# Hedgehog linear attention feeding a squared-ReLU FFN: first loads in parts, maxima subtracted in two k groups, latencies of the plan changed for batch 0

## The chip, the cores and the metric

One core of a Trainium2 chip. The metric is device microseconds for one launch. Every number called a time is the median of a kernel's runs; a span or a time of day inside a run comes from one profiled execution of that kernel, which is 1.7 to 1.9 us shorter than the time that the same execution is given.

## The reference

```python
# q, k, v: 8 batches x 8 heads x 576 x 64;  w_phi: 64 x 128
def phi(x):
    proj = einsum('bhsd,df->bhsf', x, w_phi)
    proj = proj - max(abs(proj), axis=-1, keepdims=True)
    return concatenate([exp(proj), exp(-proj)], axis=-1)
q_p, k_p = phi(q), phi(k)
kv  = einsum('bhsf,bhsd->bhfd', k_p, v)          # "KV" below
z   = sum(k_p, axis=2)
num = einsum('bhsf,bhfd->bhsd', q_p, kv)         # numerator
den = einsum('bhsf,bhf->bhs', q_p, z)[..., None] + 1e-06
x   = (num / den).transpose(0, 2, 1, 3).reshape(4608, 512)
h   = maximum(x @ w_in, 0.0)                     # FFN-in, 512 -> 2048
out = h * h @ w_out                              # FFN-out, 2048 -> 512
```

## The kernel before

All inputs are loaded from f32 to bf16. The kernel does not emit its instructions in the order of the source text. It builds operations with an engine, an estimated cost, an estimated latency, dependencies, buffers and a priority key, simulates all engines, and then emits each operation in the order in which the simulation started it, so each engine gets its instructions in that order.

```python
class Plan:
    SWITCH = 96                       # planned cost of a change between 64- and 128-row matmuls
    AHEAD, GROUP, LATE = 12, 2, 4     # when to change the row size
    def pick(self, q, rows, can): ...
    def order(self):                  # event simulation: cost, latency, free buffers, priority
        ...
                    end, lat = now + o.cost, o.lat
                    if o.rows is not None:
                        if rows[e] not in (None, o.rows):
                            end += self.SWITCH
                        rows[e] = o.rows
        ...
    MARGIN = 200
    def pe(key, cost, fn, deps=(), bufs=(), rows=128):
        o = pl.op("pe", cost, key, fn, deps, bufs, lat=350, rows=rows)
        ...
    def act(key, n, fn, deps=(), bufs=()):
        return pl.op("act", 60 + 0.83 * n, key, fn, deps, bufs, lat=220 + MARGIN)
    # dve(): lat=190 + MARGIN;  pool(): lat=150 + MARGIN
    ...
    FIRSTS = "k0 v0 q0 win k1 v1 wout q1"    # batch 0 in two halves, the rest whole
```

The exponentials of k come in five groups a batch: four of 8 units and one of 4 (a unit is 128 tokens-by-head rows of 64). There are two ways to handle the maximum. In the first, here called folding, ScalarE takes the exponential of the raw projection straight from PSUM, and the factor exp(-max) or exp(+max) is multiplied onto v instead, once for each sign. In the second, VectorE subtracts the maximum, ScalarE takes both signs of two banks in two long instructions, and v is copied once, unscaled. Before the change batches 0 and 1 fold in all five groups, and later batches subtract in all of them.

```python
    FOLD, VON = 2, ((1, 1), (0, 1))    # VON[batch][sign]: 1 = GpSimd scales v, 0 = VectorE does
    ...
        fold = b < FOLD
        if not fold:                   # plain copy of v and its column of ones, on GpSimd
            ...
        for g, (u0, n) in enumerate(GRP):
            ...                        # projection of k: 64-row matmuls into two banks
            if not fold:
                ...                    # per bank: reduce abs max, subtract -> ksh (VectorE)
                ...                    # two exponentials of 2*c (ScalarE)
                continue
            ...                        # reduce abs max (VectorE), four exponentials of c (ScalarE)
            for s_, (y, sg) in enumerate(zip(va, (-1.0, 1.0))):
                ...                    # exp(sg * max), small (ScalarE)
                on = VON[b][s_]
                def fn(y=y, u0=u0, n=n, v_=(nc.vector, nc.gpsimd)[on]):
                    v_.tensor_tensor(
                        out=y.t[:, u0 : u0 + n, :D], in0=xv.t[:, u0 : u0 + n, :],
                        in1=y.t[:, u0 : u0 + n, D].to_broadcast([P, n, D]), op=ALU.mult)
```

Where the plan leaves the tensor engine (PE) idle before the first FFN input exists, it puts a matmul on a constant tile, a filler:

```python
    def warm():
        nc.tensor.matmul(out=r_one.tiles[7][:, : 2 * Fd], lhsT=ones[:, :P], rhs=ones, ...)
    ...
    pl.fill("pe", 108, lambda now: 500 if now < 500 else 240 if now < 5500 else PER, warm, o_end)
    ...
    with tc.manual_schedule():
        for o in pl.order():
            if o.fn is not None:
                o.fn()
```

## Time and profile before

| | before |
|---|---|
| time, us (first 3 runs) | 367.8 (367.53 to 368.38) |
| span of the profiled run | 365.6 |
| PE busy, of it fillers | 353.7, 16.4 (101 fillers) |
| first FFN-in matmul at | 28.11 |
| first FFN-out matmul at | 44.80 |
| clock in 43.4 to 46.8 us | 0.50 |

PE is TensorE, PEld its weight loads, DVE is VectorE, ACT is ScalarE, POOL is GpSimd, SP is SyncE; L and a number is a line of that kernel. Line numbers differ between the kernels: folded v is scaled at L523 before and L541 after, KV is L556 and L574, the numerators L700 and L720, FFN-in L762 and L782, FFN-out L791 and L811.

The prediction below shows the page and the table by stretches. Two more views belong to the argument. The first is the chain of work that ended last, by engine; the second, the PE waits between 28 and 49 us (engine, tile and line that waited, what it waited for, total us, times, longest).

```profile
PE 82%; DVE 6%; DMA 3%; POOL 3%; SPq 2%; issue 2%; ACT 1%; DVEq 0%; POOLq 0%; ACTq 0%
```

```profile
PE one L700 <- ACT kph L508: 1.3, 2, 0.7
PE one L466 <- DVE xo L721: 0.9, 1, 0.9
PE one L762 <- ACT hr L767: 0.2, 1, 0.2
```

The chain is 82% PE; VectorE, DMA and GpSimd hold 12% of it; that is where something other than PE set the pace. No single wait between 28 and 49 us is above 0.9 us: the loss there is made of small pieces. The timeline of the same stretch (start, duration, engine, line, operation) shows who scales v in batch 1.

```profile
36.07 1.05 POOL L523 TENSOR_TENSOR va<-xv,va 128x512 bf16<-128x512 bf16 x1
...
39.67 2.52 POOL L523 TENSOR_TENSOR va<-xv,va 128x512 bf16<-128x512 bf16 x2
40.06 1.21 DVE L523 TENSOR_TENSOR va<-xv,va 128x512 bf16<-128x512 bf16 x1
```

VectorE and GpSimd do the same kind of scaling at the same time. VectorE's scaling at 36.08 (shown in the prediction, 1.59 us) began with GpSimd's of 1.05 us and ended 0.55 us after it, at 37.67; the one at 40.06 ended at 41.27, also 0.54 after GpSimd's first of the pair, which ended at 40.73 by the single records. So 0.54 us is what it costs VectorE once the other is out of the way. GpSimd waits in its turn: its second of the pair, from 40.69, took 1.50 us in place of 1.05 and ended 0.92 after VectorE's at 41.27. This is what the Trainium skill, "SBUF — State Buffer", section Who interferes with whom, says of a VectorE instruction with two SBUF inputs beside a GpSimd one that reads SBUF, and the trace agrees: 1.59 = 1.05 + 0.54.

### The profile page before, as it was taken

What the parts mean: (1) busy time and instruction counts of PE and PEld (TensorE: products, weight loads), DVE (VectorE), ACT (ScalarE), POOL (GpSimd) and SP (SyncE); (2) the same over time, 40 slices, a digit from 0 to 9 for tenths busy, and PEclk for the clock granted to TensorE, in tenths of its full rate; (3) what the DMA queues carried; (4) which work ended last, traced back from release to release, by engine and by line L of the source; (5) the groups of instructions that cost most, each with busy time, mean ns of one, the idle gap of its engine ahead of it and who ended that gap; (6) DMA issues with size and microseconds to landing.
All of it is one profiled execution on the core that took longest, in us unless ns stands there. A gap on an engine that the chain in (4) does not pass through costs nothing.

```text
span 365.6 us, 10343 instructions
## 1 busy us (share of the span) xinstructions
PE 353.7 (97%) x4069; PEld 200.0 (55%) x4069; DVE 246.5 (67%) x553; ACT 242.3 (66%) x501; POOL 186.0 (51%) x289
## 2 busy tenths in 40 slices
PE   8899799999999999999999999999999999999994
PEld 6679576766654555455545554454445544444442
DVE  2779969894789589868596868875886743332321
ACT  2997979689739983997479846985699633333300
POOL 8855745458837881787538764785445600000000
PEclk9999899999999999999999999999999999999999
DMA  7999962559755975488656944595520331121133
GB/s 110 208 209 208 208 119 59 90 85 166 133 102 81 173 147 103 87 161 157 94 102 113 176 96 100 90 216 87 109 64 22 74 82 34 29 48 41 29 72 73
DMA packets 68257, 39.81 MB, mean 109 GB/s; under 512 B 48624, under 2 KB 63088, under 8 KB 68208
## 3 DMA queue, kind: packets, MB, share of 16 engines
q0 software_dynamic: 15312, 18.35, 30.3%
q1 hardware_dynamic: 52896, 20.79, 28.7%
q8 instruction: 32, 0.52, 0.6%
q14 instruction: 17, 0.14, 0.1%
HBM read 36.77 MB, written 9.44 MB: 126 GB/s over the span
## 4 chain that ended last, share of the span: by engine, by line
PE 82%; DVE 6%; DMA 3%; POOL 3%; SPq 2%; issue 2%; ACT 1%; DVEq 0%; POOLq 0%; ACTq 0%
PE one L791 32%; PE one L762 31%; PE one L700 6%; PE one L556 4%; PE one L600 3%; PE one L632 3%; DVE mk L477 2%; POOL va L523 2%; DMA xv<-in_v_dram 2%; DVE ksh L487 2%; PE one L466 2%; SPq L401 2%; DMA qT<-xq 1%; PE one L366 1%; DVE ot L798 1%
## 5 line engine op out<-in xcount | busy, mean ns | idle before, releaser
L770 POOL TENSOR_TENSOR h<-hr 128x512 bf16<-128x512 bf16 x112 | 115.8, 1042 | 87.1 <-ACT hr L767 85.0
L762 PE MATMUL one<-xT,win 128*128 128x512 bf16 (+2 forms) x768 | 145.7, 326 | 0.9 <-DVE ksh L487 0.7
L791 PE MATMUL one<-wout,h 128*128 128x512 bf16 x576 | 145.9, 381 | 0.2 <-DVE m L653 0.2
L767 ACT ACTIVATE hr<-one 128x512 bf16<-128x512 f32 x144 | 85.3, 606 | 77.8 <-PE one L762 69.6
L762 PEld LDWEIGHTS <-win 128*128 128x128 bf16 x768 | 66.0, 98 | 50.4 <-issue 1.8
L791 PEld LDWEIGHTS <-h 128*128 128x128 bf16 x576 | 51.8, 98 | 57.3 <-issue 2.6
L607 ACT ACTIVATE qph<-one 128x512 bf16<-128x512 f32 (+1 forms) x160 | 78.0, 572 | 7.0 <-PE one L600 5.8
L495 ACT ACTIVATE kph<-ksh 128x1024 bf16<-128x1024 f32 (+1 forms) x60 | 54.9, 969 | 11.4 <-DVE ksh L487 10.9
L477 DVE TENSOR_REDUCE mk<-one 128x4 f32<-128x512 f32 (+1 forms) x80 | 49.3, 625 | 5.5 <-PE one L466 5.5
L653 DVE TENSOR_REDUCE m<-one 128x4 f32<-128x512 f32 (+1 forms) x60 | 35.5, 628 | 18.6 <-PE one L632 12.8
L798 DVE COPY ot<-one 128x512 f32<-128x512 f32 x36 | 24.7, 686 | 27.1 <-PE one L791 26.8
L710 DVE TENSOR_TENSOR one<-one,em 128x260 f32<-128x260 f32 (+1 forms) x80 | 32.0, 430 | 13.2 <-PE one L700 11.0
L487 DVE TENSOR_TENSOR ksh<-one,mk 128x512 f32<-128x512 f32 (+1 forms) x60 | 38.3, 638 | 3.3
L700 PEld LDWEIGHTS <-qph 128*128 128x128 bf16 x640 | 30.1, 98 | 16.4 <-issue 3.2
L700 PE MATMUL one<-kv_sb,qph 128*128 128x65 bf16 x640 | 34.7, 194 | 1.3 <-ACT kph L508 1.3
L721 DVE TENSOR_TENSOR xo<-one,rden 128x256 bf16<-128x256 f32 (+1 forms) x80 | 31.3, 417 | 0.6
L773 DVE TENSOR_TENSOR h<-hr 128x512 bf16<-128x512 bf16 x32 | 13.5, 422 | 23.3 <-ACT hr L767 23.3
L662 POOL COPY mq<-m 64x4 f32<-64x4 f32 x108 | 20.0, 185 | 9.4 <-DVE m L653 5.6
L556 PE MATMUL one<-va,kph 64*128 64x65 bf16 x1152 | 23.9, 191 | 0.2
L556 PEld LDWEIGHTS <-kph 64*128 64x128 bf16 x1152 | 21.2, 94 | 4.9 <-issue 4.4
L508 ACT ACTIVATE kph<-one 128x512 bf16<-128x512 f32 (+1 forms) x40 | 19.6, 605 | 2.1 <-DVE mk L477 2.1
L366 PE MATMUL one<-ones 128*128 128x256 bf16 x101 | 16.4, 305 | 1.2 <-DVE scrap L312 1.2
(46 smaller groups left out, 209.1 us busy)
## 6 DMA issues: line engine op xcount, KB each, us to landing
out_dram<-ot SPq DMA_DIRECT2D x72, 128.0 KB, 2.4
xk<-in_k_dram POOLq DMA_DIRECT2D x7, 576.0 KB, 6.4
xv<-in_v_dram POOLq DMA_DIRECT2D x7, 576.0 KB, 9.0
xq<-in_q_dram POOLq DMA_DIRECT2D x7, 576.0 KB, 11.8
win<-in_moe_w_in_dram POOLq DMA_DIRECT2D x1, 2048.0 KB, 18.8
wout<-in_moe_w_out_dram POOLq DMA_DIRECT2D x1, 2048.0 KB, 29.8
xk<-in_k_dram POOLq DMA_DIRECT2D x2, 288.0 KB, 5.3
xv<-in_v_dram POOLq DMA_DIRECT2D x2, 288.0 KB, 7.5
```

The source lines that it names most:

```text
L477: nc.vector.tensor_reduce(out=mk.t[:, e, ms], in_=wv(e), axis=AX.X, op=ALU.max, apply_absolute_value=True)
L487: nc.vector.tensor_tensor(out=ksh.t[:, e, : n // 2, :], in0=wv(e), in1=mk.t[:, e, ms].to_broadcast([P, n // 2, Fd]), op=ALU.subtract)
L495: nc.scalar.activation(out=t.t[:, :, : n // 2, :].rearrange("x e i f -> x e (i f)"), in_=ksh.t[:, :, : n // 2, :].rearrange("x e i f -> x ...
L556: nc.tensor.matmul(out=kvp(w, hi)[:, 2 * prl + s], lhsT=kph[g][s].t[r, i % 2, i // 2, :], rhs=va[s].t[r, u, : D + 1], start=(j == 0), stop ...
L607: nc.scalar.activation(out=t.t.rearrange("f (r b) hi p -> f b r hi p", b=2)[:, bk, :, :, lo:hi_], in_=w[bk].t[:, : nj * 256].rearrange("f ...
L653: d1 = [dve(kk, nj * 256, lambda w=w, m0=m0, nj=nj, bk=bk: nc.vector.tensor_reduce(out=m0.t[:, bk, : 2 * nj], in_=w[bk].t[:, : nj * 256].r ...
L700: nc.tensor.matmul(out=w.t[:, z * P : z * P + D + 1], lhsT=qg[s].t[:, h // 2, h % 2, :], rhs=kv[r][0].t[:, z % 2, z // 2, s, :], start=(s ...
L710: nc.vector.tensor_tensor(out=x, in0=x, in1=em.t[lo:hi_, hs].to_broadcast(list(x.shape)), op=ALU.mult)
L762: nc.tensor.matmul(out=w.t[:, y * n : (y + 1) * n], lhsT=win[:, kc, mc * P : (mc + 1) * P], rhs=xT.t[:, a:z, kc, :], start=(kc == 0), stop ...
L767: o = act(key - 4, TCH, lambda: nc.scalar.activation(out=r.t, in_=w.t, func=ACT.Relu), [p_], [w, r])
L770: o = pool(key - 4, 1050, lambda: nc.gpsimd.tensor_tensor(out=t.t, in0=r.t, in1=r.t, op=ALU.mult), [o], [r, t])
L791: nc.tensor.matmul(out=w.t, lhsT=h2[c, mc, tt][0].t[:, h2[c, mc, tt][1] :][:, :P], rhs=wout[:, mc, :], start=(mc == 0), stop=(mc == KC2 - 1))
```

## The change

The intent is to shorten the first 50 us. k of batch 0 arrives in a quarter, a quarter and a half, so that PE can start earlier; the FFN weights arrive in halves, the last one behind q of batch 1; the last two k groups of batch 0 are subtracted on VectorE, so that GpSimd has four scalings less; and the latencies by which the plan orders batch 0 are set to exact values in place of ones with a margin. The diff also does two things to batch 1 which its description does not name: its last two k groups are subtracted as well, and all its scalings go to GpSimd.

```diff
-    FOLD, VON = 2, ((1, 1), (0, 1))
+    KVJ = 1
+    FG, VON = (3, 3), ((1, 1), (1, 1))     # FG: groups that fold, in batches 0 and 1
...
+    M0 = 40, 200, 350
+    slack = [M0[0]]
-        o = pl.op("pe", cost, key, fn, deps, bufs, lat=350, rows=rows)
+        o = pl.op("pe", cost, key, fn, deps, bufs, lat=350 if slack[0] >= 100 else 240, rows=rows)
-        return pl.op("act", 60 + 0.83 * n, key, fn, deps, bufs, lat=220 + MARGIN)
+        return pl.op("act", ..., lat=220 - 70 * (slack[0] < 100) + slack[0])
...                                          (alike for VectorE, 190 - 60, and GpSimd, 150)
-    FIRSTS = "k0 v0 q0 win k1 v1 wout q1"
+    FIRSTS = "k0:0-1 k0:1-2 k0:2-4 v0:0-2 v0:2-4 q0:0-2 q0:2-4 win:0-8 win:8-16 k1:0-4 v1:0-4 wout:0-8 q1:0-4 wout:8-16"
+    NEXT = 9                                (loads from the tenth on get a later priority)
...
-        fold = b < FOLD
-        va = [Buf(r_va), Buf(r_va)] if fold else [Buf(r_va)] * 2
+        nf = FG[b] if b < len(FG) else 0
+        va = [Buf(r_va), Buf(r_va)] if nf else [Buf(r_va)]
...
-            if not fold:
+            if g >= nf:
...
-                                    rhs=va[s].t[r, u, : D + 1],
+                                    rhs=va[s if g < nf else 0].t[r, u, : D + 1],
...
+                    if b < KVJ:
+                        gs = {u // 8 for u in range(2 * NJ * hf, 2 * NJ * hf + 2 * NJ)}
```

With all of these undone together, the order built from the changed source is that of the kernel before, instruction for instruction, on PE, VectorE, ScalarE and GpSimd (a build, not a run), so the four parts named above, with the KVJ line, are the whole change.

## The prediction

> **What bounds the kernel now.** I read the page first (busy shares and slices), then the per-stretch table of busy times, then the timeline of the first 60 us, then the waits, then the DMA view.
>
> ```profile
> span 365.6 us, 10343 instructions
> PE 353.7 (97%) x4069; PEld 200.0 (55%) x4069; DVE 246.5 (67%) x553; ACT 242.3 (66%) x501; POOL 186.0 (51%) x289
> PEclk9999899999999999999999999999999999999999
> L366 PE MATMUL one<-ones 128*128 128x256 bf16 x101 | 16.4, 305 | 1.2 <-DVE scrap L312 1.2
> ```
>
> PE is busy 353.7 of 365.6 us, but 16.4 us of that are the 101 filler matmuls on the constant tile, so useful PE work is 353.7 - 16.4 = 337.3 us and everything else is 28.3 us. Only that remainder can be won; the change neither adds nor removes useful matmuls (the built order has 20 fillers fewer and nothing else fewer). The clock digit 8 in the fifth slice matters below. By stretches, with boundaries put at the first FFN matmul (28.1), at the beginning and end of the idle PE time, and at the end of the slow clock:
>
> ```profile
> 0.00:6.30 6.30, 5.10 (x26) 3.69 (x27) 0.66 (x5) 1.49 (x2) 5.17 (x13) 1.00 0.56 79
> 6.30:28.10 21.80, 20.05 (x377) 15.20 (x375) 15.77 (x37) 19.14 (x52) 15.05 (x17) 1.00 1.13 205
> ...
> 28.10:36.00 7.90, 7.90 (x154) 7.33 (x153) 7.57 (x17) 6.04 (x18) 4.80 (x5) 1.00 1.24 208
> 36.00:43.40 7.40, 5.01 (x90) 4.25 (x87) 7.40 (x13) 7.40 (x20) 5.56 (x6) 1.00 1.23 208
> 43.40:46.80 3.40, 3.39 (x31) 1.68 (x28) 3.40 (x12) 2.49 (x7) 2.88 (x4) 0.50 1.21 207
> 46.80:49.10 2.30, 2.30 (x145) 2.24 (x141) 1.72 (x2) 2.30 (x10) 1.07 (x2) 1.00 1.21 207
> ...
> 100.00:200.00 100.00, 99.39 (x1193) 51.25 (x1193) 78.13 (x174) 74.78 (x146) 63.70 (x106) 1.00 0.67 119
> ```
>
> Columns are busy us of PE, weight load, VectorE, ScalarE, GpSimd, then clock, DMA share, GB/s. Up to 28.1 us fillers and idle make 28.1 - (25.15 - 16.4) = 19.35 us. From 36.0 to 43.4 PE loses 2.39 us while VectorE and ScalarE are full, and then the clock is 0.50 for 3.4 us. After 49 us PE is full: about 1.5 us idle up to 300, then a tail of 4.7 us that no part of the change touches. So the program is PE bound from 49 us on; the time can change only by getting there earlier.
>
> How the two early stretches are bound, from the timeline:
>
> ```profile
> 8.59 0.56 PE L412 MATMUL one<-ident,xk 128*128 128x128 bf16 x7 [0.31 <-DMA xk<-in_k_dram]
> 10.67 1.05 POOL L523 TENSOR_TENSOR va<-xv,va 128x512 bf16<-128x512 bf16 x1 [2.15 <-DMA xv<-in_v_dram]
> 13.39 0.62 PE L412 MATMUL one<-ident,xq 128*128 128x128 bf16 x8 [1.22 <-DMA xq<-in_q_dram]
> 16.77 5.25 POOL L523 TENSOR_TENSOR va<-xv,va 128x512 bf16<-128x512 bf16 x6
> 17.30 1.33 ACT L508 ACTIVATE kph<-one 128x256 bf16<-128x256 f32 x4
> 36.08 1.59 DVE L523 TENSOR_TENSOR va<-xv,va 128x512 bf16<-128x512 bf16 x1
> 41.29 1.45 DVE L523 TENSOR_TENSOR va<-xv,va 128x512 bf16<-128x512 bf16 x1
> 44.80 1.91 PE L791 MATMUL one<-wout,h 128*128 128x512 bf16 x4
> ```
>
> The head waits for data: the second half of k at 8.5, v at 10.5, q at 13.3. In batch 1 VectorE spends up to 1.59 us on one scaling of v. The four FFN-out matmuls at 44.80 take 1.91 us, against 0.86 to 0.97 us in the steady part of the chain: the half clock.
>
> **What the Trainium skill says.** "TensorE: Matmul & The Clock Gate", Part 1: the array runs at half its clock after an idle window of about 3.4 us. The trace agrees in size (0.50 for 3.4 us) although PE was idle only 2.39 of the 7.4 us before it. "SBUF — State Buffer", Who interferes with whom: a VectorE instruction with two SBUF inputs contends with a GpSimd one that reads SBUF, the loser blocks. The scaling of v is such an instruction; its four full-size runs on VectorE average 1320 ns, with equal ones on GpSimd at 1093. I take the lock as the likely reason, not as shown. "VectorE: DVE Perf Modes", perf-mode tier table: a reduce, and a two-tensor operation that reads PSUM, run at one element a cycle; agreed, 625 and 638 ns for 128x512 in the page. "DMA: Bandwidth & Descriptors", Bandwidth: about 425 GB/s measured for a large load. Here 208 GB/s of bf16 are written from f32, so 416 are read: from 9 to 49 us the queue is full, and bytes, not pieces, set when things land.
>
> **The change part by part.**
>
> 1. k0 in three parts. The first is a quarter, not a half, of k. The half landed 4.8 us after its issue at 1.26; I estimate the quarter at 5.0 to 5.3. PE first has 22 fillers, at the 0.2 us each of the opening (27 took 5.38), so it is free at 5.6, against 6.4: 0.8 us gained on the first group. But the last part carries the same total bytes and lands at 8.5 or a little later, and group 1 now stands behind the last part's transposes in PE's order. So the gain is spent by 9.4 us.
>
> 2. Groups 3 and 4 of batch 0 by subtraction. ScalarE: group 3's four exponentials of 128x512 at 0.54 become two of 128x1024 at 0.97 (-0.2), group 4's four of 128x256 at 0.33 become two at 0.54 (-0.2), and four small ones of 0.17 go (-0.7): about -1.1 us. GpSimd: two scalings of 1.05 and two of 0.57 (3.2 us) become one plain copy of 12 units, 12/36 of 2.11 = 0.7, plus a memset: -2.4. VectorE: four subtractions, 2 x 0.64 + 2 x 0.38 = +2.0 us. Walking VectorE's new order from the reduce of group 1 at 9.45: 1.25 + copy 0.35 + 1.25 + four at 0.64 + copy 0.2 + q copy 0.69 + four at 0.39 + q copies 0.88 gives 18.2 for the last copy of q (16.8 before). The q projections then start at 18.3 (17.36 before), where ScalarE, done with k at 18.5, takes them at 18.7 (18.35 before). GpSimd has three more DMA issues of 0.75 before its first scaling (10.9 to 11.4 instead of 10.67) but then ends its v work at 18.1 to 18.6 instead of 22.0.
>
> 3. So what follows is shorter again: no matmul waits for v any more. KV's second half, 72 matmuls at 0.023, ends at 22.0; numerator matmuls at 22.4 (22.87 before); scale, reciprocal, output, transpose by the same durations as before give the first FFN matmul at 27.8 against 28.1. Head: -0.3 us, uncertain by 0.7.
>
> 4. In the diff but not in its title: in batch 1 all scalings of v go to GpSimd, and its last two groups too are subtracted. VectorE loses 1.59 + 1.21 + 1.45 + 1.79 = 6.04 us and gains 2.0: 4 us less in a stretch where it is busy 20.1 of 21.0. GpSimd gains about 3 us (six scalings and a copy, 7.2, for 4.2) there, and has room (14.3 of 21.0). The most this can return is the 2.39 us of idle plus half of the 3.4 us at 0.50, 1.7: 4.1. ScalarE is full from 36.0 to 43.4 as well and is relieved only at the last two groups, so I take about 60%: -2.5 us.
>
> 5. Weights in two. The first FFN matmul waited for nothing (weights landed at 25.0), so the first split hides. The second half of the FFN-out weight now goes behind q1 in a full queue and should land when q1 did, 15.95 + 28.3 = 44.3 us, not 41.5. PE comes to it with its third FFN-out group, which I put at 45 to 46: no cost.
>
> Sum: -0.3 - 2.5 = -2.8 us: 367.8 - 2.8 = 365.0.
>
> **Rivals.** (a) The second half of the FFN-out weight becomes the wait. For: if PE ran without any idle it would be there at about 44.9. Against: it needs everything else to go right. It caps the gain near 3.2 us. (b) VectorE in the head: 9.4 to 18.2 us without a gap. If the subtractions delay the q side by more than GpSimd gives back, the head is 1 us longer and the total about 366.3. (c) ScalarE, already full, keeps batch 1's pace; the clock still drops, and the gain is under 1 us: 367. (d) The head was really limited by planner order and the exact latencies pack it by the 4 us that the 20 missing fillers suggest (20 x 0.2): then 361 to 362. Against: k, v and q land no earlier.
>
> **Range and chances.** 365.0, with 362.9 to 366.9 eight times in ten: the top is (c), the bottom is step 4 nearly complete with 1 us more from the head. Two per cent is 7.4 us and would need twice the whole batch 1 loss, or (d) and step 4 together: 0.04. Slower by 2% needs a new stall of 7 us, for which no place is seen: 0.01. Within 2%: 0.95.
>
> **What would show it.** First FFN matmul at 27 to 28.6; no VectorE scaling of v; idle PE between 28 and 47 us under 1.3 us and no clock of 0.50 there; GpSimd's v work of batch 0 done before 19; the third FFN-out group with no wait on the weight over 0.5 us; 1.5 us of idle from 49 to 300 as before. A first FFN matmul before 26 or after 29, a second slow-clock stretch, or GpSimd releasing batch 1's KV late would make the prediction wrong.

## The result, and the profile after

| | before | after |
|---|---|---|
| time, us | 367.9 (367.53 to 368.38, 4 runs) | 363.81 (363.52 to 364.31, 4 runs) |
| ratio | 1 | 0.9889 (0.9872 to 0.9907) |
| span | 365.6 | 361.8 |
| PE busy, of it fillers | 353.7, 16.40 (101) | 351.5, 13.78 (81) |
| idle PE | 11.85 | 10.35 |
| useful PE work | 337.35 | 337.67 |
| first FFN-in / first FFN-out matmul | 28.11 / 44.80 | 25.08 / 40.50 |
| clock under 1, before the tail | 3.4 us at 0.50 | none |

A ratio, here and below, is the mean time of one kernel's fast runs over that of the other's of the same rounds, so not quite the ratio of the medians quoted; the interval is 95%. The tail is the last 4.7 us, in which PE has no more work. The change makes the kernel 1.1% faster, 4.1 us. That is inside the 2% called the same, and inside the predicted range.

The page of the changed kernel: span, busy times, granted clock, then by engine the chain that ended last.

```profile
span 361.8 us, 10273 instructions
PE 351.5 (97%) x4049; PEld 196.9 (54%) x4049; DVE 246.3 (68%) x556; ACT 241.6 (67%) x485; POOL 186.3 (52%) x293
PEclk9999999999999999999999999999999999999999
...
PE 85%; DVE 12%; issue 2%; ACT 0%; DVEq 0%
```

The digit 8 is gone from the clock. GpSimd and DMA, 3% each, are gone from the chain, and VectorE has gone from 6% to 12% of it. The fillers, from the groups of PE:

```profile
L378 PE MATMUL one<-ones 128*128 128x256 bf16 x81 | 13.8, 311 | 1.2 <-DVE scrap L316 1.2
```

Busy times by stretch, with the boundaries that the prediction used (columns: stretch, length, then PE, weight load, VectorE, ScalarE, GpSimd, clock, DMA share, GB/s), and one more line that ends where the first FFN matmul now starts:

```profile
28.10:36.00 7.90, 7.65 (x149) 6.92 (x148) 7.04 (x20) 5.36 (x14) 7.05 (x9) 1.00 1.23 207
36.00:43.40 7.40, 6.54 (x83) 4.10 (x80) 6.79 (x16) 7.40 (x22) 6.30 (x7) 1.00 1.23 207
43.40:46.80 3.40, 3.40 (x98) 3.00 (x98) 3.33 (x8) 3.40 (x6) 3.26 (x4) 1.00 1.22 209
...
100.00:200.00 100.00, 99.54 (x1214) 51.75 (x1213) 78.55 (x172) 77.10 (x153) 63.74 (x106) 1.00 0.69 123
```

```profile
0.00:25.08 25.08, 22.01 (x366) 15.89 (x366) 16.96 (x40) 18.34 (x41) 18.70 (x29) 1.00 1.00 168
```

From 36.0 to 43.4 PE now idles 7.40 - 6.54 = 0.86 us where it idled 2.39, and no half clock follows: 43.4 to 46.8 holds 98 matmuls where it held 31. In the long middle, 100 to 200 us, both kernels keep PE above 99% busy; there is nothing to win there. Up to the first FFN matmul, waiting (fillers and idle) is 25.08 - (22.01 - 13.74) = 16.81 us, against 19.35 before.

The waits of PE from 34 to 46 us:

```profile
PE one L720 <- DVE one L730: 0.5, 1, 0.5
PE one L482 <- DVE xo L741: 0.2, 1, 0.2
```

The timeline of the head, in order of time:

```profile
8.15 0.39 PE L424 MATMUL one<-ident,xk 128*128 128x128 bf16 x4
13.33 5.10 POOL L541 TENSOR_TENSOR va<-xv,va 128x512 bf16<-128x512 bf16 x5
17.12 0.88 DVE L432 COPY qT<-one 128x1024 bf16<-128x1024 bf16 x2
17.53 0.61 PE L620 MATMUL one<-qT,wphi 64*128 64x256 bf16 x4
...
19.41 1.31 PE L574 MATMUL one<-va,kph 64*128 64x65 bf16 x72
20.87 0.30 PE L720 MATMUL one<-kv_sb,qph 128*128 128x65 bf16 x4
21.07 3.04 ACT L627 ACTIVATE qph<-one 128x512 bf16<-128x512 f32 x6
23.55 0.40 PE L751 MATMUL one<-ident,xo 128*128 128x128 bf16 x4
24.27 0.58 ACT L756 ACTIVATE xT<-one 128x512 bf16<-128x512 bf16 x1
25.08 1.06 PE L782 MATMUL one<-xT,win 128*128 128x128 bf16 x16
```

The same places before:

```profile
22.87 0.29 PE L700 MATMUL one<-kv_sb,qph 128*128 128x65 bf16 x4
...
23.86 2.07 ACT L607 ACTIVATE qph<-one 128x512 bf16<-128x512 f32 x4
26.33 0.40 PE L731 MATMUL one<-ident,xo 128*128 128x128 bf16 x4
26.43 0.60 ACT L607 ACTIVATE qph<-one 128x512 bf16<-128x512 f32 x1 [0.51 <-PE one L600]
26.93 0.59 ACT L736 ACTIVATE xT<-one 128x512 bf16<-128x512 bf16 x1
```

The last chain of the head runs from the first numerator (L720, L700) by the transposes of its result (L751, L731) and their copy (L756, L736) to the first FFN matmul. The first numerator comes 2.00 us earlier (20.87 against 22.87), the transposes 2.78, the first FFN matmul 3.03. So two thirds of the lead is there before the first numerator, and one third comes after it. In that last part ScalarE has fewer exponentials of q ahead of the copy (10 in place of 13, counted on the timeline) and runs six of them without a gap, where before it stood 0.51 us for a projection.

The whole difference of the two profiled spans, as a sum:

| term, us | before | after | difference |
|---|---|---|---|
| waiting (fillers and idle) up to the first FFN matmul | 19.35 | 16.81 | -2.5 |
| idle from there to 62 us | 2.40 | 1.18 | -1.2 |
| idle after 62 us, with the tail of 4.7 | 6.50 | 6.10 | -0.4 |
| half clock: 3.4 us at 0.50, half of it lost | 1.70 | 0 | -1.7 |
| the rest of useful PE work | 335.65 | 337.67 | +2.0 |
| span | 365.6 | 361.8 | -3.8 |

The half-clock term is what PE lost in this one execution. It is not what the change won by being rid of it. The record gives the mean clock of every execution, and 3.41 us at 0.50 lower it by 0.0047. Of the 42 executions of before that were timed beside the experiments, 23 have 0.995 or less; the 19 with 0.997 or more cannot have had such a stretch. (In the traces the slow clock of the tail alone takes off at most 0.0033.) The 19 were only 0.1 us faster, with a 95% interval from 0.3 slower to 0.5 faster. So in the order of before the end of the half clock is worth at most some 0.5 us, not 1.7. Where an execution without it loses the time instead, no kept trace shows. Three stretches of the profiled execution, each 3.41 us long, show what went before the half clock:

```profile
36.57:39.98 3.41, 2.59 (x47) 2.10 (x45) 3.41 (x6) 3.41 (x10) 1.86 (x3) 1.00 1.24 208
39.98:43.40 3.42, 1.85 (x36) 1.57 (x33) 3.42 (x7) 3.42 (x10) 3.13 (x3) 1.00 1.21 208
43.40:46.81 3.41, 3.40 (x33) 1.69 (x30) 3.41 (x12) 2.50 (x7) 2.89 (x4) 0.50 1.21 207
```

The last term is mostly a cost of the new order. Its PE program changes between 64-row and 128-row matmuls 202 times, that of before 186 times. What a change costs is the excess of the start-to-start time at such a pair over the usual pace. My first figure for it was 0.124 us each, and the expectations below still use 0.12. It was too high: 64-row matmuls start in pairs (those of 64x128 some 4 ns and then 53 ns apart), and the median pace of 4 ns left the last one's own 53 ns in the excess. Against the spacing of the pairs it is 0.097 us on average in both kernels, the same in both directions (median 96 ns into 64 rows, 95 ns back), while going from one operation of 128 rows to another costs 0.002. Sixteen more changes make 16 x 0.097 = 1.6 us of the term; 0.4 us stay open.

### The profile page after: what moved, and what is told of

Read it like the earlier page. It is cut to its first block, busy times and chain, and to the rows that moved or that the text cites. A ratio compares the mean times of both kernels' runs of the same rounds, so it can differ in the third digit from the quotient of the medians.

```text
span 361.8 us, 10273 instructions
## 1 busy us (share of the span) xinstructions
PE 351.5 (97%) x4049; PEld 196.9 (54%) x4049; DVE 246.3 (68%) x556; ACT 241.6 (67%) x485; POOL 186.3 (52%) x293
## 4 chain that ended last, share of the span: by engine, by line
PE 85%; DVE 12%; issue 2%; ACT 0%; DVEq 0%
PE one L811 32%; PE one L782 31%; PE one L720 6%; DVE mk L493 5%; PE one L574 5%; DVE ksh L503 3%; PE one L620 3%; PE one L652 3%; PE one L482 2%; PE one L378 2%; DVE ot L818 1%; PE one L424 1%; DVE m L659 1%; DVE xo L741 1%; DVE one L730 0%
## 5 line engine op out<-in xcount | busy, mean ns | idle before, releaser
L811 PEld LDWEIGHTS <-h 128*128 128x128 bf16 x576 | 51.0, 97 | 56.6 <-issue 1.9
L511 ACT ACTIVATE kph<-ksh 128x1024 bf16<-128x1024 f32 (+1 forms) x68 | 60.9, 953 | 11.1 <-DVE ksh L503 10.6
L673 DVE TENSOR_REDUCE m<-one 128x4 f32<-128x512 f32 (+1 forms) x60 | 35.5, 629 | 19.8 <-PE one L652 15.9
L503 DVE TENSOR_TENSOR ksh<-one,mk 128x512 f32<-128x512 f32 (+1 forms) x68 | 42.8, 629 | 3.5
L720 PEld LDWEIGHTS <-qph 128*128 128x128 bf16 x640 | 30.4, 97 | 17.8 <-issue 3.1
L720 PE MATMUL one<-kv_sb,qph 128*128 128x65 bf16 x640 | 35.4, 194 | 0.6 <-DVE one L730 0.5
L737 DVE RECIPROCAL rden<-one 128x4 f32<-128x4 f32 (+1 forms) x80 | 12.4, 174 | 9.1 <-PE one L720 8.4
L659 DVE TENSOR_REDUCE m<-one 128x4 f32<-128x512 f32 (+1 forms) x20 | 13.0, 684 | 4.3 <-PE one L652 4.2
```

The lines of the kernel that those rows point to most:

```text
L503: nc.vector.tensor_tensor(out=ksh.t[:, e, : n // 2, :], in0=wv(e), in1=mk.t[:, e, ms].to_broadcast([P, n // 2, Fd]), op=ALU.subtract)
L511: nc.scalar.activation(out=t.t[:, :, : n // 2, :].rearrange("x e i f -> x e (i f)"), in_=ksh.t[:, :, : n // 2, :].rearrange("x e i f -> x ...
L673: d1 = [dve(kk, nj * 256, lambda w=w, m0=m0, nj=nj, bk=bk: nc.vector.tensor_reduce(out=m0.t[:, bk, : 2 * nj], in_=w[bk].t[:, : nj * 256].r ...
L720: nc.tensor.matmul(out=w.t[:, z * P : z * P + D + 1], lhsT=qg[s].t[:, h // 2, h % 2, :], rhs=kv[r][0].t[:, z % 2, z // 2, s, :], start=(s ...
L811: nc.tensor.matmul(out=w.t, lhsT=h2[c, mc, tt][0].t[:, h2[c, mc, tt][1] :][:, :P], rhs=wout[:, mc, :], start=(mc == 0), stop=(mc == KC2 - 1))
```

## The experiments

All were made to tell these theories apart. A: GpSimd's scalings of batch 0 held the head, and the subtraction frees it. C: VectorE's scalings of batch 1, which block on GpSimd's, made the idle time and the half clock. The rivals: the parts of the loads made the difference; or the new latencies did, by the order that they give; or the removed fillers themselves were the gain (J). The expectations name their theories by such letters.

There are two kinds of kernel. The first kind leaves one part of the change out and lets the plan order everything again. The second kind keeps the planned order of one kernel exactly and changes only what one instruction is when it is emitted, so only the hardware answers. Most traces of the second kind lack about 1% of the matmul records, so their idle time over long stretches is not compared.

### Leaving one part out

Subtraction in batch 0 left out (a_fold0):

```diff
-    FG, VON = (3, 3), ((1, 1), (1, 1))
+    FG, VON = (5, 3), ((1, 1), (1, 1))
```

> The changed kernel with only batch 0's subtraction undone (all five k groups scale v on GpSimd again). Theory A (the head was gained because GpSimd's ten scalings of v held the KV matmuls until 22 us and now end at 18.4): most of the head's lead of about 2.4 us goes back, 365.8 to 366.3 us; GpSimd's last scaling of v in batch 0 ends at 21 us or later and the first FFN matmul comes at 27 us or later. Rival B (the exact planner latencies made the head): under 0.7 us lost, about 364.3, first FFN matmul still near 25.3.

Exact latencies left out (a_lat):

```diff
-    M0 = 40, 200, 350
+    M0 = 200, 200, 350
```

> The changed kernel with the old planner latencies (margin 200) in batch 0. Rival B (exact latencies packed the head): 2 us or more lost, about 366, first FFN matmul at 27 or later. Theory A (GpSimd chain): under 0.8 us lost, 363.9 to 364.6, since 16 more fillers at 0.11 us in the way cost at most 1.8 us and partly fill idle time.

Batch 1 as it was, five folded groups and one sign on VectorE (a_b1):

```diff
-    FG, VON = (3, 3), ((1, 1), (1, 1))
+    FG, VON = (3, 5), ((1, 1), (0, 1))
```

> The changed kernel with batch 1 as before (scalings of v on VectorE for one sign, no subtraction). Theory C (batch 1's VectorE load made idle PE and the half clock between 36 and 47 us): head the same (first FFN matmul at 25.1), then over 1.5 us more idle or a clock of 0.5 in 33 to 45 us, 365.3 to 366.3 us. Rival D (the earlier head alone shifted everything; batch 1's load is hidden): within 0.5 us of the changed kernel, 363.5 to 364.3.

Loads as they were (a_loads):

```diff
-    FIRSTS = "k0:0-1 k0:1-2 k0:2-4 v0:0-2 v0:2-4 q0:0-2 q0:2-4 win:0-8 win:8-16 k1:0-4 v1:0-4 wout:0-8 q1:0-4 wout:8-16"
-    NEXT = 9
+    FIRSTS = "k0:0-2 k0:2-4 v0:0-2 v0:2-4 q0:0-2 q0:2-4 win:0-16 k1:0-4 v1:0-4 wout:0-16 q1:0-4"
+    NEXT = 99
```

> The changed kernel with the old loads (k0 in two parts, both weights whole, old order). Theory E (bytes in a full queue, not pieces, set the landing): within 0.6 us, 363.8 to 364.4. Rival F (the quarter of k and the earlier FFN weight half are worth having): 1 us or more lost, 364.9 or more, with the first group's transposes at 6.4 instead of 5.75 and its lead kept to the first FFN matmul.

Measured, all four beside the same runs of before (367.78), with what their profiles hold (us; "changes" are changes of the row size on PE):

| | time | ratio to before | first FFN-in | first FFN-out | useful PE work | idle 0 to 62 | idle after, tail left out | changes |
|---|---|---|---|---|---|---|---|---|
| before | 367.78 | 1 | 28.11 | 44.80 | 337.35 | 5.35 | 1.81 | 186 |
| after | 363.81 | 0.9889 | 25.08 | 40.50 | 337.67 | 4.25 | 1.38 | 202 |
| a_fold0 | 364.65 | 0.9917 (0.9905 to 0.9930) | 28.31 | 41.85 | 337.06 | 5.17 | 1.67 | 198 |
| a_lat | 366.99 | 0.9985 (0.9973 to 0.9997) | 26.44 | 38.70 | 337.88 | 4.07 | 3.24 | 204 |
| a_b1 | 367.70 | 1.0000 (0.9988 to 1.0013) | 25.64 | 41.26 | 337.21 | 6.15 | 4.34 | 194 |
| a_loads | 371.49 | 1.0128 (1.0095 to 1.0161) | 27.61 | 47.95 | 341.93 | 5.21 | 4.02 | 216 |

(The after row is from the first result; before was 367.9 there.)

The four losses against after are 0.8, 3.2, 3.9 and 7.7 us; together 15.6, nearly four times the 4.1 that the whole change gives. So the parts cannot be added up: each of these kernels is a different order of everything. What can be read from them is where each lost its time.

a_fold0 loses the whole lead of the head: the first FFN matmul is back at 28.31. The timeline of its GpSimd and PE:

```profile
13.24 8.29 POOL L541 TENSOR_TENSOR va<-xv,va 128x512 bf16<-128x512 bf16 x9
...
28.31 1.07 PE L782 MATMUL one<-xT,win 128*128 128x128 bf16 x16
```

GpSimd scales v until 21.5 us, against 18.43 after, and the plan put 15 exponentials of q ahead of the copy. Yet the start of the FFN, 3.2 us later than after's, costs only part of that: fillers and idle time up to 62 us are 19.98 us (14.81 + 5.17) against 18.03 (13.78 + 4.25), 1.95 more, with 0.6 us less useful work, and the medians differ by 0.84. Theory A had the marks of the head right (27 us or later) and the total wrong (365.8 or more). The start of the FFN is not by itself what sets the end; how PE is filled until about 62 us is.

a_lat has the first FFN-out matmul earliest of all, at 38.70, and still loses 3.2 us: idle time after 62 us is 1.9 us larger and the head 1.4 us longer. Only the plan's latencies differ here, so these 3.2 us are the order's alone.

a_b1 keeps most of the lead of the head (25.64) and has no half clock in the profiled execution (two of the other four have a mean clock of 0.994 and 0.995), but it idles 1.9 us more before 62 us and 3.0 more after, and the whole gain is gone. When the plan orders all again, batch 1's part, which the description of the change does not name, is needed for any gain at all.

a_loads is the surprise, 7.7 us slower than after, far outside what theory E allowed and more than F asked for. Its first FFN-out matmul and its middle:

```profile
47.95 1.04 PE L811 MATMUL one<-wout,h 128*128 128x512 bf16 x4
```

```profile
100.00:200.00 100.00, 96.84 (x1070) 49.27 (x1067) 75.89 (x173) 70.58 (x135) 59.66 (x99) 1.00 0.69 114
```

FFN-out starts only at 47.95, 3.2 us later than even in the kernel before with the same loads, and PE then idles 3.16 of the 100 us from 100 to 200, against 0.46 after. Its useful work also takes 4.3 us longer; 14 more changes of the row size explain 1.4 of these, and the rest stays open.

### The same pieces of loads with the order kept

f_a_oldload keeps the order of after, but the first k part loads half of k and the second nothing, and each weight is loaded whole where its first half stood.

```diff
+        whole = b == 0 and name == "k" and a < 2
+            if whole and a == 1:
+                return                        # the second part does nothing
+            if whole:
+                z = 2                         # the first loads both
-                out=win[:, :, x], in_=win_v[:, :, x]))
+                out=win, in_=win_v) if a == 0 else None)
                 (the same for wout)
```

> The changed kernel with its order kept; only the pieces of the loads are the old ones: the first k part carries a half, both weights are loaded whole in the place of their first part. Theory E (bytes, not pieces; the 371.5 us of the earlier run with the old loads came from the new planned order): 363.3 to 364.6, first FFN matmul at 25.1 to 25.8. Rival F (the pieces themselves matter): 366 or more. The whole FFN-out weight, ahead of q1, should land about 42 us, so the first FFN-out matmul at 40.5 may wait 1 to 2 us for it: then up to 365.5.

It took 363.97 us, ratio to before 0.9911 (0.9887 to 0.9934), against 0.9889 for after. The first FFN-in matmul was at 25.33 and the first FFN-out at 40.76, each within 0.3 us of after's, although the whole FFN-out weight landed only at 40.1. So no worth of the pieces as pieces is shown: 0.2 us by the medians, 0.8 by the ratios, whose intervals overlap. This fits what the prediction concluded from a queue that read 416 GB/s, beside about 425 for a large load in the Trainium skill, "DMA: Bandwidth & Descriptors", section Bandwidth: bytes, not pieces, set the landing. What a_loads lost, it lost through the order that the plan built from the other pieces and priorities, not through the pieces.

### Who scales v in batch 1

f_a_va1dve keeps the order of after and gives the three scalings of one sign in batch 1 back to VectorE:

```diff
-  v_=(nc.vector, nc.gpsimd)[on]
+  v_=(nc.vector, nc.gpsimd)[on and not (b == 1 and s_ == 0)]
```

> The changed kernel with its order kept; only batch 1's three scalings of v for one sign run on VectorE again. Theory C: 1.0 to 3.0 us slower than the changed kernel, 364.8 to 366.8, with the loss as idle PE or half clock between 35 and 46 us and the head untouched. Theory G (in the earlier run that undid batch 1 most of the loss came from the new planned order, not from VectorE): within 0.7 us of the changed kernel, 363.2 to 364.5.

It took 366.12 us, 0.9948 (0.9928 to 0.9967): 2.3 us slower than after's 363.81, more than half of the gain lost. Its stretches and its one large wait:

```profile
36.00:40.00 4.00, 2.73 (x54) 2.53 (x55) 4.00 (x8) 3.92 (x12) 2.84 (x3) 1.00 1.23 207
40.00:44.00 4.00, 3.51 (x28) 1.85 (x29) 3.86 (x10) 3.27 (x9) 1.47 (x2) 0.62 1.24 209
```

```profile
PE one L720 <- DVE one L730: 1.3, 1, 1.3
```

VectorE is full from 36 to 40 us, the numerator's wait for VectorE grows from 0.5 to 1.3 us, and the lowered clock is back, 0.62 in the mean of 40 to 44 us. VectorE's three scalings took 1.41, 0.68 and 0.86 us. Theory C holds for the order of after as to the time and the idle PE: these three instructions alone cost about 2 us. The slow clock is not the reason for most of it. Three of the six executions had it (mean clock 0.992 to 0.994) and took 366.02 to 366.52 us; the three without (0.999 to 1.000) took 365.11, 365.13 and 366.41, all at least 1.3 us above after. One mark was missed: the head was not untouched, the first FFN matmul came at 25.60 in place of 25.08, though nothing of batch 0 was changed.

f_b_va1pool is the counterpart: the order of before, with all scalings of batch 1 on GpSimd.

```diff
-  v_=(nc.vector, nc.gpsimd)[on]
+  v_=(nc.vector, nc.gpsimd)[on or b == 1]
```

> The kernel before with its order of instructions kept; only batch 1's five VectorE scalings of v run on GpSimd, in the same places. Theory C (VectorE's load in batch 1 made the idle PE time and then the half clock): no clock of 0.5 left, idle PE between 36 and 44 us under 1.2 instead of 2.4 us, 2 to 3.5 us faster than before (364.3 to 365.8). Rival D (ScalarE was just as full and keeps the pace): idle and half clock stay, within 0.7 us of before.

It took 369.24 us, 1.0046 (1.0020 to 1.0071): slower, by 1.4 us, where theory C expected 364.3 to 365.8. Two stretches, the wait and its place:

```profile
36.00:43.40 7.40, 5.84 (x104) 4.98 (x101) 5.33 (x14) 7.40 (x21) 6.86 (x7) 1.00 1.23 209
47.00:50.00 3.00, 0.56 (x35) 0.45 (x30) 0.00 (x0) 2.11 (x9) 3.00 (x4) 1.00 1.20 205
```

```profile
49.63 1.46 PE L556 MATMUL one<-va,kph 64*128 64x65 bf16 x60 [2.44 <-POOL va L523]
```

VectorE does have time now (5.33 of 7.40 us busy, it was full), PE's idle time falls to 1.56 us, and no half clock follows in this execution (three of the other five have a mean clock of 0.994 or 0.995). But GpSimd has ten scalings to do, and KV waits 2.44 us for the last of them. So in this order the move alone does not pay; in the changed kernel it comes with the subtraction, which takes four scalings off GpSimd. The subtraction of batch 1 without the move was not run.

### Does GpSimd hold the head?

f_b_va0copy asks that of the order of before. Batch 0's scalings of v are replaced by copies of the same shape, which are faster. The result is wrong (relative error 0.045).

```diff
+                    if b == 0:
+                        v_.tensor_copy(out=y.t[:, u0 : u0 + n, :D], in_=xv.t[:, u0 : u0 + n, :])
+                        return
```

> The kernel before with its order kept; in batch 0 GpSimd only copies v instead of scaling it (wrong result on purpose). A copy of 128x768 took 0.83 us in the changed kernel's profile, so about 0.55 for 128x512 against 1.05: 4 to 4.5 us less GpSimd work before the last KV matmul. Theory A (this GpSimd work held the head): last KV matmul of batch 0 at 21.3 us or earlier instead of 22.2, first FFN matmul 0.7 us or more earlier, total 0.5 to 1.5 us less. Rival B (PE's planned order with its fillers was as late as GpSimd): first FFN matmul within 0.4 us of 28.1, total within 0.5 us.

It took 367.16 us beside 367.67 for before, 0.9986 (0.9969 to 1.0002). Its timeline:

```profile
15.24 2.95 POOL L524 COPY va<-xv 128x512 bf16<-128x512 bf16 x6
...
28.04 1.07 PE L765 MATMUL one<-xT,win 128*128 128x128 bf16 x16
```

GpSimd is through with v at 18.2 us in place of 22.0, and the first FFN matmul is at 28.04 in place of 28.11. Theory A by itself falls: in the order of before, work of GpSimd is not what holds the head. With a_fold0, which has the loads and latencies of the change but all the scalings and no lead at all, this says that the head needs the subtraction and an order that uses it. What in the subtraction counts is not shown: it relieves GpSimd, but by the prediction's estimate it also takes 1.1 us off ScalarE, and no run separates the two.

f_b_va0dve, with the order of before and the scalings of batch 0's groups 3 and 4 on VectorE, was meant as another way to relieve GpSimd.

```diff
-  v_=(nc.vector, nc.gpsimd)[on]
+  v_=(nc.vector, nc.gpsimd)[on and not (b == 0 and g > 2)]
```

> The kernel before with its order kept; only batch 0's four last scalings of v run on VectorE instead of GpSimd. Theory A (GpSimd's scalings of v held the KV matmuls of the head): last KV matmul at 21 us or earlier instead of 22.4, first FFN matmul 0.7 to 1.7 us earlier, total 0.7 to 1.7 us less. Rival B (GpSimd did not bind the head, the planned order and its fillers did): first FFN matmul within 0.4 us of 28.1 and the total within 0.5 us.

It took 368.37 us, 1.0018 (0.9998 to 1.0038). Two of the scalings on VectorE:

```profile
16.39 3.31 DVE L523 TENSOR_TENSOR va<-xv,va 128x512 bf16<-128x512 bf16 x2
```

They took 3.31 us beside GpSimd's. The two of group 3 came 1.2 to 1.6 us earlier for it, but the last v only at 21.90 in place of 22.03, and the last KV matmul started at 22.24, where it was 22.19. As a test of theory A this is inconclusive, since the end of v was hardly moved. It shows the same contention as before, on two more instructions.

### Are the fillers a gain by themselves?

f_a_nofill keeps the order of after and emits no filler after the 65th.

```diff
+    warmed = []
     def warm():
+        warmed.append(0)
+        if len(warmed) > 65:
+            return
```

> The changed kernel with its order kept, and the 16 fillers left out that stand between batch 0's second group of KV matmuls (18.9 us) and the first FFN matmul (25.1). PE is busy 99% of 18 to 26 us there, 16 fillers at 0.11 are 1.8 us. Theory J (the fillers stand in PE's way in the head, and the 20 that the exact latencies dropped are what the head gained): first FFN matmul 0.7 to 1.8 us earlier than 25.1 and the total 0.5 to 1.5 us less, 362.3 to 363.3. Rival K (the fillers only fill waits for VectorE and ScalarE): first FFN matmul within 0.4 us of 25.1 and the total within 0.4 us of the changed kernel, idle PE in place of the fillers; or the half clock comes back and it is slower.

It took 363.42 us, 0.987 (0.9848 to 0.9891), against 0.9889 (0.9872 to 0.9907) for after: the intervals overlap. PE in its head:

```profile
23.31 0.38 PE L657 MATMUL one<-wphi,qT 64*128 64x128 bf16 x7 [0.37 <-ACT qph L632]
...
24.93 1.05 PE L787 MATMUL one<-xT,win 128*128 128x128 bf16 x16
```

```profile
18.00:26.00 8.00, 7.23 (x196) 5.55 (x194) 7.08 (x18) 7.98 (x21) 2.70 (x4) 1.00 1.15 210
```

Sixteen fillers fewer, and the first FFN matmul is at 24.93 in place of 25.08; the waits show as waits, and the clock stays 1.00. Fillers lie in time that is lost anyway, so theory J falls and rival K holds: the 20 missing fillers of the change are a sign of less waiting, not its cause. ScalarE is busy 7.98 of these 8 us, so I take it to pace this stretch after the change; no run tests that.

### Can the changes of the row size be had back?

The +2.0 us of the sum suggest a better version. Two tries with the changed kernel: s_g38 lets the plan wait for larger groups of 64-row matmuls, and s_sw250 tells it that a change costs 250 ns.

```diff
-    AHEAD, GROUP, LATE = 12, 2, 4
+    AHEAD, GROUP, LATE = 12, 3, 8       # s_g38
```

> The changed kernel with a planner that gathers more 64-row work before it changes the row size (16 changes fewer, 186 for 202; the head has the same order). Theory H (each change of row size costs PE about 0.12 us beyond the matmuls, which is why useful busy time did not fall although the half clock went): 1.0 to 2.5 us faster than the changed kernel, 361.3 to 362.8. Rival: the later 64-row work makes new waits that eat it, 363.3 to 364.5.

```diff
-    SWITCH = 96
+    SWITCH = 250                        # s_sw250
```

> The changed kernel with the planner told that a change of row size costs 250 ns instead of 96 (174 changes instead of 202, 67 fillers instead of 81, a somewhat different head). Theory H: 28 changes at 0.12 are 3.4 us, so 360.0 to 362.0. Rival: the plan with a wrong cost runs away from the chip and adds idle time, 363 or more.

s_g38 took 363.80 us, 0.9899 (0.9881 to 0.9917). It has 186 changes, 16 fewer, but its useful PE work fell by only 0.4 us, and idle PE rose by 1.2 (11.5 against 10.35). Nothing is gained. s_sw250 took 373.83 us, 1.0164 (1.0142 to 1.0187), with 174 changes. From 62 us to the tail:

```profile
62.00:342.40 280.40, 270.31 (x2943) 144.62 (x2942) 189.09 (x425) 187.04 (x359) 143.80 (x237) 1.00 0.55 99
```

PE idles 10.1 us there, against 1.4 after. So in these two plans taking changes away cost at least as much in waits. No kernel that I ran beats after clearly; f_a_nofill is within its noise.

## Why the prediction was right or wrong

The predicted time was 365.0 and the measured 363.81, a gain of 4.1 us for a predicted 2.8. That the total came so near was in part luck: the head gained 2.2 us more than predicted, and a term that the sum lacked took 2.0 back. By its own list of signs the prediction was wrong in the head, since the first FFN matmul came "before 26".

**Step 1, k0 in three parts: right.** PE's first group started at 5.75 us (predicted 5.6) against 6.41, and the last part's transposes ran at 8.15, so that the lead was spent by about 9 us. f_a_oldload shows no gain of the pieces at the end.

**Step 2, the balance of the engines: right in what it walked.** VectorE's last copy of q ended at 18.00 (predicted 18.2), GpSimd's v work at 18.43 (18.1 to 18.6).

**Step 3, the head at -0.3: the step that failed.** It was mis-sized: waiting in the head fell by 2.5 us, and the first FFN matmul came at 25.08, not 27.8. Three numbers of it are at fault. "The q projections then start at 18.3" took the last copy of q as their release; they needed only the one before, and started at 17.53. "72 matmuls at 0.023, ends at 22.0" had their pace from a kernel in which they were interleaved and waited; in one piece they took 1.31 us, 0.018 each, and ended at 20.72. And "by the same durations as before" took the 5.24 us from the first numerator to the first FFN matmul as fixed; it was 4.21, with ScalarE's order changed. The walk followed the data; the order of the other engines was read too little, though it was known. Rival (d), that the order limited the head, named this. Its argument against itself, that k, v and q land no earlier, did not bear on it: the waiting that went away came after all three had been waited for. Fillers and idle time up to 13.4 us are 11.4 before and 11.3 after, from 13.4 to 17.0 they are 2.25 and 2.44, and from 17.0 to the first FFN matmul 5.66 (17.0 to 28.11) and 3.05 (17.0 to 25.08). How much of it is the count of exponentials ahead of the copy (13 before, 10 after) I read from traces only; no run isolates it. a_b1 and a_loads also have 10 but start FFN at 25.64 and 27.61, so the count alone is not it.

**Step 4, batch 1 at -2.5: right for the idle time, not shown for the half clock.** Idle time from the first FFN matmul to 62 us fell by 1.2, and none of the four executions of after has a half clock. But the 1.7 us that the prediction counted among what could return is not in the times: executions of before without a half clock took 0.1 us less. f_a_va1dve shows that VectorE's scalings cost about 2 us, a_b1 that this part is needed, f_b_va1pool that the move alone is not enough. Two readings were low: GpSimd's five scalings of batch 1, put at 4.2 us, took 5.3 by the single records, 0.45 of it waiting for VectorE; and the idle time from 49 to 300 us was 1.8, not 1.5. Rival (c), that a full ScalarE keeps the pace, fell: ScalarE is still full from 36.0 to 43.4 (7.40 of 7.40), and PE idles 0.86 us.

**Step 5, the weights: right, by a wrong reason.** The second half of the FFN-out weight landed at about 45.0 us, near the 44.3 predicted. The third FFN-out group ran at 42.53, before that and without a wait, since the plan had put a group that needs the first half only in its place. Rival (a), a wait for that half, did not come.

**A term that the sum lacked:** +2.0 us of other useful work, 1.6 of it the order's 16 more changes of the row size. The prediction said that useful work would stay the same, and counted with the half clock it did (337.35 and 337.67). With the term the working reads -2.5 - 1.2 - 0.4 - 1.7 + 2.0 = -3.8 in the profiled spans.

**Rival (b)**, VectorE delaying the q side by more than GpSimd gives, did not come either: the projections of q started at 17.53 against 17.36, 0.2 us later.

What stays open: which detail of ScalarE's order makes the lead of the head, whether GpSimd's relief or ScalarE's made it possible, and the 2.9 us of extra useful work in a_loads that the changes of the row size do not explain.

## What to carry to other kernels

Where a planner orders the instructions, read the built order on every engine before predicting, and don't take a duration between two events from the old order: the parts of such a change do not add up, and one that seems idle (the pieces of a load) can decide the result through the plan. Moving work from a full engine to one with room pays only if the receiving engine still delivers in time; here the move alone was slower, and the move came with fewer scalings in the kernel that gained. Don't count a stretch of half clock as time to be won before looking at executions that lack it. To tell hardware from order, keep the order and change single instructions.

## What the Trainium skill lacked or had wrong

- "TensorE: Matmul & The Clock Gate", Part 1, gives an idle window of about 3.4 us before the clock is halved; the page has no figure for how much idle time in a window is enough. I counted stretches of 3.41 us from the first clock record of each of the 14 traces (5.85 us in that of before) up to 340 us. PE was busy 1.74 to 1.88 us in the four that a half clock followed (before, f_a_va1dve, f_b_va0copy, f_b_va0dve). It was busy 1.98 us or more in all others but one, of 1.85 in f_b_va1pool, where the trace has only three of the four FFN-out matmuls at 44.70. So here a stretch that PE filled to some 55% was enough, and one of 58% was not. A wait of 2.44 us in f_b_va1pool did no harm; it lay across two such stretches. The first record came at 3.9 to 7.0 us, so the stretches lie differently in each execution, which would explain why only 23 of 42 executions of before had a half clock.
- "TensorEngine Tiling (Array Packing)", section Key Properties, says that a change of the tiling mode drains the TensorE, without a cost. Here a change between 64-row and 128-row matmuls cost 0.097 us on average (183 changes measured before, 198 after).
- "SBUF — State Buffer", section Who interferes with whom, was right; it has no durations for this operation. A scaling of 128x512 in bf16 took VectorE 0.54 us beyond GpSimd's, 1.59 us when it waited for one of GpSimd's of 1.05, and 0.68 with none beside it (f_a_va1dve).
